# A fourth weight buffer, late list puts three a step, and the first batch's pooled remainder in the prologue of an attention and two-MoE kernel

## The chip, the cores and the metric

The kernel runs on 1 core of one Trainium2 chip. The metric is the device time of one execution in microseconds; lower is better. Before the change it is 747.93 us, the median of 3 runs.

## What is computed

An attention block is followed by two mixture-of-experts (MoE) layers. Cut to what matters:

```python
# q, k, v: (4, 8, 576, 64); factor = 4
q_d, k_d, v_d = (mean of each 4 neighbouring positions of q, k, v)
out_up = repeat(softmax(q_d k_d^T / 8) v_d, 4)           # pooled attention
out_local = softmax(q k^T / 8 where |i - j| < 4) v       # banded attention
x = out_up + out_local                                   # as 2304 rows of 512
x = moe(x, w_gate, w_output_gate, w1, w2)                # 8 experts, one per row
out = moe2(x, w_gate, w1, w2)

def moe(x, ...):
    e = argmax(x @ w_gate);  g = softmax(x @ w_gate)[e]
    y = relu(x @ w1[e]) @ w2[e]                          # 512 -> 1024 -> 512
    return g * sigmoid(x @ w_output_gate)[e] * y         # moe2 has no sigmoid
```

## The kernel before

**Attention** goes through 4 batches of 5 tiles, 20 tiles in all, in a loop over steps s (L818). In step s tile s gets its banded scores, tile s - 1 its probabilities transposed, its products with v and its 512 values a token (`xevac`, L681, which also stores the rows to `x0` in DRAM on SP's queue, two stores of at most 58 rows a tile), and tile s - 2 its gate logits (`xflip`, `lmm`, `lsel`). The pooled part of a batch is five `Pooled` objects: c = 0 to 3 take the first 128 pooled queries of a pair of heads, c = 4 the remainder, the last 16 to 32 of all pairs, in four column groups of TensorE. Each goes through `scores` (L502, the remainder's at L517 to L528) and `smax`, `exps`, `flip` and `evac`, `pvs` and `norm`. For later batches they are spread over the steps by `pooled_at` (L722). For batch 0, c = 0 to 3 are in the prologue, whose order is written out in `PRO` (s, m and f with a number stand for scores to exponential, transposes, and products with the norm); its remainder is in step `REM0` = 0 and the step after. GpSimd (POOL) makes the sums over four positions. The pooled v of a batch (`vpd`, L488) is needed by `pvs`.

**Routing.** When a group of tiles (`GROUPS`) has its logits, `route` (L256) finds each token's expert and place, and `spread` and `put` add the tokens to a list in PSUM: per tile `spread` makes `am`, `oc` and `bm` (L349 to L355; `bm` has two buffers, and `PB` says how many of its three parts are ACT operations at L353), and `put` is one matmul (L362). `ready1` and `puts1` (L836, L841) do one put and one spread a step, and `PUTN` = 2 of each from step 16 on. At the end of step 18 (`SNAP`) the tokens of the first 14 tiles are in the list, and `early` starts the first expert's work on 256 of them: `snap` picks the expert, `fetch` gathers the rows (`gather`, L1154) into `xr`, of which there are five buffers, and `prime` starts the weight loads. The tokens of the last six tiles come into the list after that; `rank` then orders the experts and a second `fetch` gathers 256 more rows for the second job, with the same weights.

**Experts.** `jobs` go through the experts of both layers. A job transposes its gathered rows (`xpose`, L1197: TensorE at L1206, ACT's upper half `xh` at L1216, VectorE's lower half `xl` at L1219), computes 8 hidden blocks (`hide`, three matmuls a product at L1294 to L1296; relu at L1420 and L1421), then the second layer. Each weight of 128 x 1024 is loaded on SP (`load_w`, L1085) into `raw`, of which there are `NRAW` = 3, split by `split_next` into `wh` (ACT cast, L1127) and `wl` (VectorE subtraction, L1135), and so gives its buffer free. `load_next` (L1095) issues a load when fewer than `NRAW` are loaded and not split. The weights of one expert are c = 0 to 7 in the stream, the first four for the first layer.

**Order.** The program order gives priorities, and a scheduler fixes each engine's instruction order before the run; each engine then works in order. Two ties are written by hand in `split_next`: the cast of c = 0 goes behind the last token's copy (`front`), the cast of c = `PINX` behind the first job's `xh` (`after`), and the subtraction of c = `PINX` behind the last tokens' places (`placed`, L326). The transposes of the first job go behind the last tokens' logits (`last`).

The engines are TensorE (PE), VectorE (DVE), ScalarE (ACT), GpSimd (POOL) and SyncE (SP, which issues the direct DMAs here). The functions that the diff touches:

Of the kernel before, what the change touches and what calls it, by code (L numbers as in the profile page):

```python
# [9 lines left out]
F32 = mybir.dt.float32  # L10
# [11 lines left out]
NP = H // 2  # L22
SD = S // 4
# [5 lines left out]
DM = 512  # L29
# [5 lines left out]
MAGIC = 12582912.0  # L35
NOV = 32
NWB = 9
NRAW = 3

CAPS = (  # L40
    (512, 384, 352, 320, 304, 288, 272, 256),
# [6 lines left out]
NWE = 3  # L48
POOLSPLIT = 0
POOLHI = 0  # L50
REM0 = 0
PUTN = 2
PB = (3, 2, 3, 2, 1)
PUTS = 15
PRI = 100
# [8 lines left out]
XA = 99  # L64
STEPF = {}
RLATE = 0
PINX = 4
QPE = 2
KPOOL = 0
Q1POOL = 0  # L70
S1 = "pppp"
PRO = "F0 s0 V0 s1 F2 s2 s3 zq m1 Ls m0 m2 f0 f1 lqk lvr f2 m3 V1 A0 lcs rep A2 f3 Le lvw zp lw1"
ORDER = "R As Ae q0f Cf Xt Cp p0s Xl Xs An p0e q1f p1s q0p Cx D p1e K q1p S"

C_ID = 0
# [105 lines left out]
def moe_pair_kernel(  # L181
# [212 lines left out]
    def attention(actx, early, early_x, front):  # L394
# [100 lines left out]
        class Pooled:  # L495
# [6 lines left out]
            def scores(self):  # L502
                b, c = self.b, self.c
                ps = psx.tile([128, 512], F32, tag="m", name="s")
                sv = ps[:, 0:2 * SD].rearrange("p (s k) -> p s k", s=2)
                if c < NP:
                    if b == 0 and c < QPE:
                        src = qt[b % 3][:, c, 0:512].rearrange("p (t r) -> p t r", r=4)
                        for r in range(4):
                            nc.tensor.matmul(  # L510
                                sv, lhsT=src[:, :, r], rhs=kpd[b % 2][:, :, c, :],
                                start=(r == 0), stop=(r == 3),
                            )
                    else:
                        nc.tensor.matmul(sv, lhsT=qd[b][:, c, 0:128], rhs=kpd[b % 2][:, :, c, :])
                else:
                    for a in range(NP):  # L517
                        if b == 0 and a < QPE:
                            src = qt[b % 3][:, a, S - 128:S].rearrange("p (t r) -> p t r", r=4)
                            ls = [src[:, :, r] for r in range(4)]  # L520
                        else:
                            ls = [qd[b][:, a, SD - 32:SD]]
                        for i, l in enumerate(ls):
                            nc.tensor.matmul(
                                sv[32 * a:32 * a + 32], lhsT=l,
                                rhs=kpd[b % 2][:, :, a, :], tile_position=(0, 32 * a),
                                start=(i == 0), stop=(i == len(ls) - 1), skip_group_check=True,
                            )  # L528
                self.sv = sv

            def smax(self):
# [190 lines left out]
        for b in range(B):  # L722
            s0 = NTP * (b - 1) + 2
            for c in range(NP + 1):
                if b or c == NP:
                    pooled_at.setdefault(s0 + c // 2 if b else REM0, []).append(Pooled(b, c))
        groups = GROUPS
        lgs_of = {}
        for g0, gn in groups:
# [29 lines left out]
        for i in range(3):  # L759
            t = sb3.tile([128, 3, 128], F32, tag="p", name="p")  # L760
            nc.sync.dma_start(t, crep[:, 3 * i:3 * i + 3])
            stg.append(t)
        c0 = [Pooled(0, c) for c in range(NP)]

        def start(c):
            c0[c].scores()
# [41 lines left out]
            "A0": lambda: sums1(0),  # L808
            "A2": lambda: sums1(2),
        }  # L810
        for c in range(NP):
            pro.update({
                f"s{c}": lambda c=c: start(c), f"m{c}": lambda c=c: middle(c), f"f{c}": lambda c=c: finish(c),
            })
# [155 lines left out]
    def experts():  # L970
# [7 lines left out]

        def pools_early():
            pool("raw", NRAW)  # L980
            pool("xr", 5)
            pool("x0")
            pool("w0", NWE)
            pool("h0")
# [181 lines left out]
        def fetch(job, fresh=None):  # L1166
# [10 lines left out]
            seen = tiles // NTP * S + tiles % NTP * 2 * GQ  # L1177
            x = []
            for k, mm in job.slots:
                xr = pl["xr"].tile([128, DM], F32, tag="xr", name="xr", bufs=5)  # L1180
                gather(M, xr, ri, k, mm, seen if job is M0.jobs[0] else NT)
                x.append(xr)
            job.x = x
# [121 lines left out]
        def overflow_slot(M, m, nov, i):  # L1305
# [39 lines left out]
            nc.vector.scalar_tensor_tensor(  # L1345
                ri[:, 0, 1:2], rf[:, 0, 0:1], -1.0, bg, op0=ALU.add, op1=ALU.add
            )
            xr = pl["xr"].tile([128, DM], F32, tag="xr", name="xr", bufs=5)
            gather(M, xr, ri, 0, 128)
            pt = psx.tile([128, 4, 128], F32, tag="m", name="t")  # L1350
            for d in range(4):
# [282 lines left out]
```

## Time and profile before

| | us |
|---|---|
| median of 3 runs | 747.93 |
| lowest, highest | 747.17, 748.26 |
| the profiled execution's own time | 742.5 |
| its span, first to last instruction | 740.7 |
| PE busy | 697.6 |
| DVE busy | 446.3 |
| ACT busy | 343.5 |
| POOL busy | 184.6 |

All times in the rows are microseconds from the start of the span, in the one profiled execution. A row of a timeline tells start, duration, engine, line, operation, what it writes and reads, shape and count; brackets at its end tell how long the engine stood idle just before and what ended that. PE's busy time contains waiting inside its pipeline.

### The profile page before, as it was taken

To read this page: it belongs to the slowest core of one execution; us is meant where nothing else is said; L and a number is where in the kernel's file an instruction comes from. 1 tells how busy PE (TensorE), PEld (TensorE's weight loads), DVE (VectorE), ACT (ScalarE), POOL (GpSimd) and SP (SyncE) were. 2 spreads that over 40 slices of the span, in tenths; PEclk is the share of its full clock that TensorE was granted. 3 is DMA by queue.
4 is the path that set the end of the run, shared out by engine and by line. 5 is a ranking of instruction groups with operands and counts; after the bars stand their busy time and mean duration, and the time that the engine had idled before them with its cause. 6 is when DMAs were issued, how large, how long until landed. Compare 5 with 4: busy or idle time off the path is not lost. (4 is left out here: it accounts for less than half of the span.)

```text
span 740.7 us, 15853 instructions
## 1 busy us (share of the span) xinstructions
PE 697.6 (94%) x6048; PEld 637.4 (86%) x6048; DVE 446.3 (60%) x1160; ACT 343.5 (46%) x634; POOL 184.6 (25%) x227
## 2 busy tenths in 40 slices
PE   8799899976989999999999999989999999999993
PEld 5468677765989999999999999878999999999992
DVE  7486979785667656575766776645444444555520
ACT  4055657584255353545454554155335354554620
POOL 5994720010131203121130130142013030321211
PEclk9699999996999999999999999999999999999998
DMA  9945553143176435445555461366435354565500
GB/s 354 420 140 210 184 196 132 55 156 131 58 247 207 160 121 183 140 161 179 173 176 168 141 221 59 110 213 217 128 111 182 126 186 141 176 193 178 163 21 16
DMA packets 52990, 120.99 MB, mean 163 GB/s; under 512 B 4800, under 2 KB 26176, under 8 KB 51884
## 3 DMA queue, kind: packets, MB, share of 16 engines
q1 hardware_dynamic: 45772, 99.19, 39.9%
q0 software_dynamic: 7136, 20.72, 8.2%
q8 instruction: 50, 0.82, 0.5%
q14 instruction: 32, 0.26, 0.1%
HBM read 101.01 MB, written 20.71 MB: 164 GB/s over the span
## 5 line engine op out<-in xcount | busy, mean ns | idle before, releaser
L1135 DVE TENSOR_TENSOR wl<-raw,wh 128x1024 fp32r<-128x1024 f32 x128 | 156.2, 1224 | 115.7 <-ACT wh L1127 115.4
L1127 ACT CAST wh<-raw 128x1024 fp32r<-128x1024 f32 x128 | 133.2, 1048 | 197.7 <-PE py L1295 113.3
L1294 PE MATMUL ph<-xh,wh 128*128 128x256 f32 (+8 forms) x576 | 172.3, 307 | 6.6 <-ACT xh L1216 6.6
L1295 PE MATMUL ph<-xl,wh 128*128 128x256 f32 (+8 forms) x576 | 175.6, 307 | 0.0
L1296 PE MATMUL ph<-xh,wl 128*128 128x256 f32 (+8 forms) x576 | 174.8, 305 | 0.0
L1294 PE MATMUL py<-h,wh 128*128 128x256 f32 (+8 forms) x448 | 138.4, 316 | 0.0
L1295 PE MATMUL py<-h,wh 128*128 128x256 f32 (+8 forms) x448 | 137.8, 311 | 0.0
L1296 PE MATMUL py<-h,wl 128*128 128x256 f32 (+8 forms) x448 | 137.4, 310 | 0.0
L1294 PEld LDWEIGHTS ph<-xh,wh 128*128 128x128 f32 x576 | 108.1, 190 | 8.4 <-ACT xh L1216 7.2
L1296 PEld LDWEIGHTS ph<-xh,wl 128*128 128x128 f32 x576 | 109.2, 190 | 0.6
L1295 PEld LDWEIGHTS ph<-xl,wh 128*128 128x128 f32 x576 | 109.1, 189 | 0.7
L1421 DVE SCALAR_TENSOR_TENSOR h<-ph,h 128x256 fp32r<-128x256 f32 (+8 forms) x144 | 66.2, 471 | 39.2 <-ACT h L1420 38.7
L1420 ACT ACTIVATE h<-ph 128x256 fp32r<-128x256 f32 (+8 forms) x144 | 60.7, 423 | 56.2 <-PE ph L1296 55.0
L1295 PEld LDWEIGHTS py<-h,wh 128*128 128x128 f32 x448 | 84.1, 188 | 0.6
L1296 PEld LDWEIGHTS py<-h,wl 128*128 128x128 f32 x448 | 84.1, 188 | 0.6
L1294 PEld LDWEIGHTS py<-h,wh 128*128 128x128 f32 x448 | 83.4, 188 | 0.9
L1156 POOL DMA_INDIRECT xr<-x,ri x49 | 50.3, 1026 | 97.1 <-PE t L1206 76.8
L1222 POOL DMA_INDIRECT out<-yr,ri x25 | 25.8, 1032 | 128.6 <-ACT yr L1240 84.2
L1222 POOL DMA_INDIRECT x<-yr,ri x24 | 25.1, 1044 | 126.3 <-ACT yr L1240 118.2
L1216 ACT CAST xh<-t 128x512 fp32r<-128x512 f32 (+5 forms) x49 | 26.1, 533 | 25.6 <-PE t L1206 25.5
L1494 DVE COPY yT<-py 128x256 f32<-128x256 f32 (+8 forms) x28 | 13.7, 490 | 39.9 <-PE py L1296 39.9
L1219 DVE TENSOR_TENSOR xl<-t,xh 128x512 fp32r<-128x512 f32 (+5 forms) x49 | 30.1, 620 | 10.5 <-ACT xh L1216 10.3
(194 smaller groups left out, 1041.8 us busy)
## 6 DMA issues: line engine op xcount, KB each, us to landing
raw<-w_a SPq DMA_DIRECT2D x64, 512.0 KB
raw<-w_b SPq DMA_DIRECT2D x64, 512.0 KB
vraw<-vr SPq DMA_DIRECT2D x4, 1560.0 KB
vd<-vw SPq DMA_DIRECT2D x4, 1280.0 KB
kd<-kT SPq DMA_DIRECT2D x8, 586.0 KB
qt<-qT SPq DMA_DIRECT2D x8, 586.0 KB
x<-zx SPq DMA_DIRECT2D x6, 768.0 KB
x<-x SPq DMA_DIRECT2D x36, 116.0 KB
```

The costliest lines, as they stand in the source:

```text
L1127: i = nc.scalar.copy(hi, raw)
L1135: i = nc.vector.tensor_tensor(lo, raw, hi.bitcast(F32), op=ALU.subtract)
L1156: g = nc.gpsimd.indirect_dma_start(xr[0:mm], None, src, bass.IndirectOffsetOnAxis(ap=ri[0:mm, k, 0:1], axis=0))
L1216: i = nc.scalar.copy(xh[:, :, o], pt[:, :, 0:mm])
L1219: nc.vector.tensor_tensor(xl[:, :, o], pt[:, :, 0:mm], xh[:, :, o].bitcast(F32), op=ALU.subtract)
L1222: i = nc.gpsimd.indirect_dma_start(M.dst[:, :], bass.IndirectOffsetOnAxis(ap=ri[0:mm, k, 1:2], axis=0), yr[0:mm], None, bounds_check=NT - ...
L1294: nc.tensor.matmul(ps, lhsT=ah, rhs=bh, start=first, stop=False)
L1295: nc.tensor.matmul(ps, lhsT=ah, rhs=bl, start=False, stop=False)
L1296: nc.tensor.matmul(ps, lhsT=al, rhs=bh, start=False, stop=last)
L1420: nc.scalar.activation(a[:, 0:n], ph[:, 0:n], func=AF.Relu)
L1421: nc.vector.scalar_tensor_tensor(b_[:, 0:n], ph[:, 0:n], 0.0, a[:, 0:n].bitcast(F32), op0=ALU.max, op1=ALU.subtract)
L1494: nc.vector.tensor_copy(yT[:, dc, 0:n], py[:, 0:n])
```

## The change

- `NRAW` goes from 3 to 4: four weight buffers. `xr` goes from five buffers to four.
- `PINX` goes from 4 to 3: the cast of the fourth weight (c = 3) goes behind the first job's `xh`, and its subtraction behind `placed`. The weight c = 4 loses these two ties.
- `PUTN` goes from 2 to 3: from step 16 on, up to three puts and three spreads a step.
- The remainder of batch 0 leaves steps 0 and 1 (`REM0` is removed) and enters the prologue as s4, m4, f4: its scores after the transposes of c = 2, its transposes after those of c = 3, its products behind the products of c = 3.
- The matmuls of the remainder's scores are issued in turns over the four column groups, instead of one group after the other. For batches after the first this leaves the order as it was.

```diff
-NRAW = 3
+NRAW = 4
...
-REM0 = 0
-PUTN = 2
+PUTN = 3
...
-PINX = 4
+PINX = 3
...
-PRO = "F0 s0 V0 s1 F2 s2 s3 zq m1 Ls m0 m2 f0 f1 lqk lvr f2 m3 V1 A0 lcs rep A2 f3 Le lvw zp lw1"
+PRO = "F0 s0 V0 s1 F2 s2 s3 zq m1 Ls m0 m2 s4 f0 f1 lqk lvr f2 m3 m4 V1 A0 lcs rep A2 f3 f4 Le lvw zp lw1"
...
+                    ls = []
                     for a in range(NP):
                         if b == 0 and a < QPE:
                             src = qt[b % 3][:, a, S - 128:S].rearrange("p (t r) -> p t r", r=4)
-                            ls = [src[:, :, r] for r in range(4)]
+                            ls.append([src[:, :, r] for r in range(4)])
                         else:
-                            ls = [qd[b][:, a, SD - 32:SD]]
-                        for i, l in enumerate(ls):
-                            nc.tensor.matmul(
...
+                            ls.append([qd[b][:, a, SD - 32:SD]])
+                    for i in range(4):
+                        for a in range(NP):
+                            if i < len(ls[a]):
+                                nc.tensor.matmul(
+                                    sv[32 * a:32 * a + 32], lhsT=ls[a][i],
...
-                if b or c == NP:
-                    pooled_at.setdefault(s0 + c // 2 if b else REM0, []).append(Pooled(b, c))
+                if b:
+                    pooled_at.setdefault(s0 + c // 2, []).append(Pooled(b, c))
...
-        c0 = [Pooled(0, c) for c in range(NP)]
+        c0 = [Pooled(0, c) for c in range(NP + 1)]
...
-            pool("xr", 5)
+            pool("xr", 4)
...
-                xr = pl["xr"].tile([128, DM], F32, tag="xr", name="xr", bufs=5)
+                xr = pl["xr"].tile([128, DM], F32, tag="xr", name="xr", bufs=4)
```

## Rows read from the trace of the kernel before

**Rows 1.** Stretch; us busy of PE, PEld, DVE, ACT, POOL; granted clock, DMA share, GB/s.

```profile
20.00:30.00 10.00, 5.86 (x22) 4.89 (x23) 4.50 (x10) 0.89 (x2) 9.48 (x12) 0.50 1.02 415
...
160.00:170.00 10.00, 5.42 (x73) 3.83 (x72) 8.67 (x40) 5.82 (x11) 2.66 (x5) 0.67 0.59 178
170.00:180.00 10.00, 3.70 (x15) 2.96 (x14) 4.95 (x22) 5.40 (x12) 0.00 (x0) 0.50 0.43 155
...
500.00:700.00 200.00, 200.00 (x1266) 191.58 (x1265) 98.67 (x131) 93.28 (x146) 39.62 (x45) 1.00 0.53 167
```

**Rows 2.** Timeline of PE at the border of attention and experts.

```profile
169.15 1.11 PE L1206 MATMUL t<-ident,xr 128*128 128x128 f32 x4 [0.37 <-DMA xr<-x,ri]
176.19 1.44 PE L1294 MATMUL ph<-xh,wh 128*128 128x256 f32 x5 [5.92 <-ACT xh L1216]
```

**Rows 3.** Timeline of ACT in the same stretch.

```profile
174.60 1.04 ACT L1127 CAST wh<-raw 128x1024 fp32r<-128x1024 f32 x1 [5.20 <-DMA raw<-w_a]
175.56 0.58 ACT L1216 CAST xh<-t 128x512 fp32r<-128x512 f32 x1
...
178.32 1.03 ACT L1127 CAST wh<-raw 128x1024 fp32r<-128x1024 f32 x1
...
181.43 0.20 ACT L309 ACTIVATE ez<-zs 128x2 f32<-128x2 f32 x1
```

**Rows 4.** Timeline of DVE from there on.

```profile
175.68 1.23 DVE L1135 TENSOR_TENSOR wl<-raw,wh 128x1024 fp32r<-128x1024 f32 x1 [4.98 <-ACT wh L1127]
...
185.47 0.16 DVE L326 TENSOR_TENSOR key<-key,cs 128x2 f32<-128x2 f32 x1
...
185.74 3.49 DVE L1135 TENSOR_TENSOR wl<-raw,wh 128x1024 fp32r<-128x1024 f32 x3
```

**Rows 5.** Timeline of SP's issues: the first weight loads and the last row stores.

```profile
153.25 1.55 SPq L1088 DMA_DIRECT2D raw<-w_a  x3
159.17 3.89 SPq L690 DMA_DIRECT2D x<-x  x4
165.61 21.82 SPq L1088 DMA_DIRECT2D raw<-w_a  x5
```

**Rows 6.** The same for single microseconds: stores alone, weights moving, before the late cast.

```profile
152.00:153.00 1.00, 0.93 (x12) 0.73 (x13) 0.97 (x4) 1.00 (x4) 0.00 (x0) 1.00 0.13 49
...
156.00:157.00 1.00, 1.00 (x24) 0.96 (x24) 0.76 (x2) 1.00 (x4) 0.00 (x0) 1.00 1.02 391
...
174.00:175.00 1.00, 0.00 (x0) 0.00 (x0) 0.00 (x0) 0.40 (x1) 0.00 (x0) 0.50 0.13 53
```

**Rows 7.** DMA issues: what, from where, count, size of one.

```profile
raw<-w_a SPq DMA_DIRECT2D x64, 512.0 KB
...
x<-x SPq DMA_DIRECT2D x36, 116.0 KB
```

**Rows 8.** Timeline of PE at the border of the two expert layers.

```profile
484.29 0.66 PE L1206 MATMUL t<-ident,xr 128*128 128x128 f32 x4 [1.81 <-DMA xr<-x,ri]
```

**Rows 9.** The second job's two gathers: the second issue, the landing times, PE's use.

```profile
198.66 0.94 POOL L1156 DMA_INDIRECT xr<-x,ri  x1 [0.31 <-issue]
...
DMA to landing us min/median/max: 3.4/3.8/4.1
...
202.90 0.60 PE L1206 MATMUL t<-ident,xr 128*128 128x128 f32 x4
```

**Rows 10.** Timelines of PE and POOL: batch 0's remainder, batch 1's pooled v and remainder.

```profile
30.38 3.99 PE L524 MATMUL s<-kpd,qt 128*32 128x288 f32 x13
...
35.03 0.39 PE L659 MATMUL v<-odh,rep 128*128 128x256 f32 x1
...
49.61 5.20 POOL L488 TENSOR_TENSOR vpd<-vraw 64x260 f32<-64x260 f32 x6
...
55.72 1.06 PE L564 MATMUL v<-vpd,pts 128*128 128x130 f32 x8
...
60.00 0.69 PE L524 MATMUL s<-kpd,qd 128*32 128x288 f32 x8
```

More of the change, by code (lines that the diff above doesn't have):

```diff
@@ L519, in scores @@
                             src = qt[b % 3][:, a, S - 128:S].rearrange("p (t r) -> p t r", r=4)
-                            ls = [src[:, :, r] for r in range(4)]
+                            ls.append([src[:, :, r] for r in range(4)])
                         else:
-                            ls = [qd[b][:, a, SD - 32:SD]]
-                        for i, l in enumerate(ls):
-                            nc.tensor.matmul(
[L525 to L528, printed above, removed]
+                            ls.append([qd[b][:, a, SD - 32:SD]])
[4 more added lines that the diff above has]
+                                    sv[32 * a:32 * a + 32], lhsT=ls[a][i],
+                                    rhs=kpd[b % 2][:, :, a, :], tile_position=(0, 32 * a),
+                                    start=(i == 0), stop=(i == len(ls[a]) - 1), skip_group_check=True,
+                                )
                 self.sv = sv
@@ L810, in attention @@
         }
-        for c in range(NP):
+        for c in range(NP + 1):
             pro.update({
@@ L1347, in overflow_slot @@
             )
-            xr = pl["xr"].tile([128, DM], F32, tag="xr", name="xr", bufs=5)
+            xr = pl["xr"].tile([128, DM], F32, tag="xr", name="xr", bufs=4)
             gather(M, xr, ri, 0, 128)
```

## The prediction

> **What bounds the kernel now.** I began with the table of busy time by stretch. TensorE (PE) is nearly always busy; the hole worth having is the border between attention and the first expert layer: in 160 to 180 us PE works 5.42 + 3.70 = 9.1 of 20 us, and the granted clock falls to 0.50, the lower of its two levels [rows 1]. The timeline of PE says where: the second transpose of the first job's rows runs at 169.15 us, and the first expert product (`hide`) starts at 176.19, after 5.92 us of idleness ended by ACT's `xh` (L1216) [rows 2].
>
> Next ACT's own timeline. The `xh` that PE waits for ran at 175.56, right behind a weight cast (L1127) that had stood 5.20 us for its load [rows 3]. ACT works in order: the fourth weight (c = 3) stood ahead of rows ready since about 170.3 (169.15 + 1.11). VectorE (DVE) stood too: its subtraction for the same weight waited 4.98 us, and the placing of the last tokens is queued behind it [rows 4].
>
> Why was that load late? SP issued three loads from 153.25, and the next only at 165.61, when the first buffer came free; between them lie the last row stores of attention (L690) [rows 5]. Ahead of the first load, while stores alone run, DMA is 0.13 busy at 49 GB/s: 0.13 of 16 is two engines; with weights moving it is 1.02 and 391 GB/s; at 174 to 175 us, with the fourth load still not landed, it is 0.13 and 53 GB/s again [rows 6]. So I read that this load ended on the two engines that the stores of 116 KB had held. A weight of 512 KB puts 32 KB on each of 16 engines, 64 KB on those two: 64 / 53 = 1.2 us each [rows 7]. Later PE has hardly a gap (500 to 700 us: 200.0 of 200, [rows 1]), but for the border between the two expert layers (1.81 us for the gathered rows, [rows 8]).
>
> **The change part by part.** All sums are against the profiled execution: 742.5 us, of which 740.7 are the span. The median of the runs is 747.93, 5.4 above it; I carry the difference over to it unchanged.
>
> *Fourth buffer and `PINX` = 3.* The fourth load is issued right behind the first three, some 11 us earlier, ahead of the last stores: at 391 GB/s 1.3 us more of transfer, then 1.2 us on the two engines. It is there before 169. Its cast is tied behind both `xh`, its subtraction behind the last tokens' places (`placed`). The later weights have no tie of their own, but in this trace they kept their order: the cast of c = 5 was over at 179.35 (178.32 + 1.03), yet no subtraction ran until that of c = 4, tied to `placed` (key at 185.47), opened the row of three at 185.74 [rows 3, 4]. So I expect c = 4 and later behind c = 3. Then `xh` runs at about 170.3, and PE starts at 170.3 + 0.6 = 170.9: 5.3 us earlier than 176.19. That is the upper end of this part.
>
> *What is late next.* The load that waited for the first free buffer still does; it is now that of c = 4. It is issued at 165.6 as before, behind the same stores, and one more weight lies on the two engines: it lands at 174.6 + 1.2 = 175.8. Its cast takes the place of the second cast after `xh` (178.32 in the trace); from there to the last tokens' second exponential (L309 at 181.43) are 3.11 us of ACT work [rows 3]. So that exponential comes at 175.8 + 3.1 = 178.9, only 2.5 us earlier. Queued behind this cast on ACT are the list's `bm`, that exponential and the first relu; DVE waits for the exponential before it places the last tokens, the list waits for them, and the second job's rows wait for the list. Those rows have no slack: the second gather is issued at 198.66, lands 4.1 us later at 202.8, and PE transposes it at 202.90 [rows 9]. With the list 2.5 us earlier they land at 200.3; PE, 5.3 us ahead, would be there at 197.6 and waits 2.7. The tied subtraction of c = 3 is needed for the seventh of eight `hide` steps; with `placed` at 183.0 (185.47 - 2.5) plus 1.2 it is ready at 184.2, about when PE comes to it, and what it costs lies inside the same 2.7. Between 2.5 and 5.3 I take the end that the two rows with the least slack give, -2.5.
>
> *Late puts, three a step.* Same spreads and puts, so no work is added; list buffers stay two, so the third spread starts when the first put is done. It can bring the first list, and gathers, up to about 1 us earlier (one spread is three ACT operations). PE cannot use it fully: rows go behind the last tokens' logits, and the hold on job 2 above is later anyway. I take 0, bounds -1 and +0.5 (a spread in front of a last tile's copy on ACT).
>
> *Remainder of batch 0 in the prologue.* Before, its scores (L524) run on PE from 30.38 to 35.03, 4.65 us, at the lower clock for the most part, with tile 0's first product (L659) queued behind [rows 10]. In 20 to 30 us PE is busy for 5.86 of 10 us and waits for POOL's pooled v [rows 1], so earlier scores are covered; were there no cover they would cost the same 4.65. Interleaving lets the four column groups work side by side, as batch 1's 8 do in 0.69 us [rows 10]; it shortens only what is hidden. The remainder's transposes and products still have to go before tile 0, some 1.5 us, and tile 0 needs the fourth pair's result at about 32. So 2.5 us at most are gained at 35 us. They meet POOL: the pooled v of batch 1 is finished at 49.61 + 5.20 = 54.81, and PE takes its last part at 55.72 [rows 10], a slack of 0.9. POOL's work is unchanged. Bounds 0 and -2.5 (PE can do other tiles meanwhile); I take -0.9, what the nearest row allows. DVE and ACT gain nothing in sum: the same operations, earlier.
>
> *Four row buffers (`xr`) instead of five.* A gather waits a transpose longer, with a whole job to spare; 0. *More loads ahead in the expert stages:* PE runs without gaps there, 0; at the second border one more load may stand ahead of the gathered rows, 0 to +1.3 (one load at 391 GB/s).
>
> [...]
>
> **Sum.** -2.5 - 0.9 = -3.4: 739.1 us profiled, 747.9 - 3.4 = **744.5 us** median. Its own range is 742.8 to 746.4.
>
> **The rivals.**
> A. *Nothing holds job 2.* If the fifth cast is queued behind the last exponential, or lands sooner, the whole 5.3 stands. For it: DVE's subtractions from c = 3 on are out of the way of the last tokens. Against it: casts stood between the list's work in the trace [rows 3]. 5.3 + 0.9 = 6.2 gives 741.7; with the prologue's 2.5, 740.1.
> B. *The wait is not removed.* If the fifth cast, which no tie holds, is queued between the two `xh`, as the fourth was, PE starts when it did. It speaks for this that its load is released at the same moment as the fourth's was; against it, that the later casts kept their order. With the prologue's 0.9 and nothing else: 747.0; up to 748 without.
> C. *Slower: one more weight stands ahead of what is waited for.* Same place as B, but the load lands 1.2 us later than before (175.8 against 174.6), and the second border's rows stand behind one more load, +1.3: 742.5 + 2.5 = 745.0, median 750.4; with the prologue's 0.9 749.5. It decides as soon as the fifth cast goes ahead of the second `xh` and the rows of the second border land later than for PE's 484.29 [rows 8].
>
> **How the numbers follow.** Forecast 0.50, A 0.22, B 0.17, C 0.11. A measurement of this kernel can tell about 0.2%, 1.5 us, from no change: under 746.4 is faster, over 749.4 slower. Faster: nearly all of the first two and a little of B, 0.73. Same: 0.16. Slower: 0.11. The range runs from the best of A (740.0) to 749.2, between B and C.
>
> **What would show it.** Right: a fourth load issued beside the three near 155 us; both `xh` together before 172, `hide` starting at about 171, ACT standing for a load until about 176 behind them, job 2's second transpose with a wait of some 2 us near 200, and L524 of batch 0 before 30 us. If that last wait is missing, it is A; if `xh` still stands until 175, B or C. What would make me wrong altogether: an order of DVE or ACT that puts a tied subtraction ahead of the last tokens, or a PE hole at 40 to 60 us where POOL is waited for longer than before.

## The result and the profile after

The changed kernel takes 751.15 us (median; 749.42 to 754.11), the kernel before beside it 746.43 us (745.51 to 748.26): a ratio of 1.0066, 95% interval 1.0049 to 1.0084. Forecast were 744.5 us, at most 749.2, and slower by over 0.2% had a chance of 0.11. The kernel became slower by some 4.7 us.

| | before | after |
|---|---|---|
| median | 746.43 us | 751.15 us |
| span of the profiled execution | 740.7 us | 748.6 us |
| time of the profiled execution | 742.5 us | 750.43 us |
| mean granted clock of TensorE | 0.972 | 0.966 |

The profiled executions differ by 7.9 us, more than the medians: that of the kernel before lies 3.9 us under its median, that of the kernel after 0.7. A part of the difference is stretches at a lower clock that a kernel of the old time shows too (0.83 as the mean of 10 us; below, at the run of the puts alone).

The table of stretches of the kernel after, to hold against [rows 1] (columns as there: stretch, length, busy time of PE, PEld, DVE, ACT, POOL with counts, granted clock, DMA share, GB/s), and under it three stretches of the kernel before that [rows 1] does not have:

```profile
50.00:60.00 10.00, 8.63 (x41) 7.98 (x41) 4.74 (x13) 1.89 (x4) 7.50 (x9) 0.66 0.45 160
170.00:180.00 10.00, 8.40 (x37) 7.46 (x37) 4.40 (x21) 3.75 (x7) 0.00 (x0) 0.55 0.50 181
200.00:215.00 15.00, 11.09 (x75) 9.60 (x74) 3.36 (x12) 3.82 (x7) 5.62 (x10) 0.77 0.47 150
485.00:500.00 15.00, 10.60 (x62) 9.31 (x61) 3.36 (x8) 4.59 (x8) 8.36 (x14) 0.77 0.62 205
```

```profile
50.00:60.00 10.00, 9.03 (x123) 7.50 (x121) 8.60 (x22) 4.55 (x10) 7.22 (x8) 1.00 0.98 363
200.00:215.00 15.00, 13.03 (x116) 12.42 (x115) 5.54 (x16) 5.96 (x12) 4.46 (x6) 1.00 0.59 192
485.00:500.00 15.00, 14.14 (x108) 13.51 (x109) 8.31 (x14) 8.02 (x14) 5.87 (x8) 1.00 0.66 196
```

What the change was for did happen: in 170 to 180 us PE is busy for 8.40 us instead of 3.70. But at 50 to 60, 200 to 215 and 485 to 500 us the granted clock is 0.66, 0.77 and 0.77 where before it was 1.00 (means over the stretch; taken in slices of 1 us it is 0.50 or 1.00 in all but 7 of 740 slices before and all but 12 of 740 after), and PE issues 41 matmuls instead of 123, 75 instead of 116, 62 instead of 108.

**A ledger of the 7.9 us**, made of the same five events in both traces. (1) The second transpose of the first job's rows, the end of attention: 171.54 against 169.15, +2.4. (2) The transpose of job 2's second rows: 205.09 against 202.90, so −0.2 in the border itself. (3) The first transpose at the second border: 488.71 against 484.29, +2.2 more. (4) The first expert product behind it: 493.03 against 486.52, +2.1 more. (5) The end of the span: 748.6 against 740.7, +1.4 more. The forecast had −0.9, −2.5, 0, 0 to +1.3, and 0.

**First border.** PE, ACT, DVE and POOL of the kernel after, to hold against [rows 2, 3, 4, 9]. A row is start, length, engine, line, operation, tiles, and in brackets the idle time before it and what ended it.

```profile
171.54 1.12 PE L1208 MATMUL t<-ident,xr 128*128 128x128 f32 x4 [0.35 <-DMA xr<-x,ri]
173.33 1.43 PE L1296 MATMUL ph<-xh,wh 128*128 128x256 f32 x5 [0.68 <-ACT xh L1218]
...
205.09 0.66 PE L1208 MATMUL t<-ident,xr 128*128 128x128 f32 x4 [1.37 <-DMA xr<-x,ri]
```

```profile
173.18 1.05 ACT L1129 CAST wh<-raw 128x1024 fp32r<-128x1024 f32 x1
178.37 1.05 ACT L1129 CAST wh<-raw 128x1024 fp32r<-128x1024 f32 x1 [4.14 <-DMA raw<-w_a]
179.32 0.72 ACT L352 ACTIVATE bm<-oc,v 128x144 fp32r<-128x144 f32 x2
179.94 1.03 ACT L1129 CAST wh<-raw 128x1024 fp32r<-128x1024 f32 x1
...
181.61 1.03 ACT L1129 CAST wh<-raw 128x1024 fp32r<-128x1024 f32 x1
182.54 0.20 ACT L308 ACTIVATE ez<-zs 128x2 f32<-128x2 f32 x1
```

```profile
186.22 0.15 DVE L325 TENSOR_TENSOR key<-key,cs 128x2 f32<-128x2 f32 x1
186.29 1.22 DVE L1137 TENSOR_TENSOR wl<-raw,wh 128x1024 fp32r<-128x1024 f32 x1
...
188.17 3.49 DVE L1137 TENSOR_TENSOR wl<-raw,wh 128x1024 fp32r<-128x1024 f32 x3
```

```profile
200.94 0.95 POOL L1158 DMA_INDIRECT xr<-x,ri  x1 [0.31 <-issue]
```

The fourth weight's cast (173.18) no longer stands ahead of `xh`, and the first product follows the transpose at once. The fifth weight's load, as forecast, is late in its stead: its cast waits 4.14 us with `bm` and the last exponential behind it. New is what DVE does after `key`: four subtractions (c = 3 and, behind one short operation of the ranks, three more) before the ranks go on, where [rows 4] had three.

**Prologue.** PE of the kernel after at 41 to 62 us and at 89 us, and POOL, to hold against [rows 10]; then three rows of the kernel before.

```profile
41.69 0.39 PE L611 MATMUL s<-cb 128*128 128x256 bf16 x2 [0.97 <-DVE p L632]
50.13 0.75 PE L514 MATMUL s<-kpd,qd 128*128 128x288 f32 x2 [0.88 <-DVE pd L538]
52.12 0.36 PE L661 MATMUL v<-odh,rep 128*128 128x256 f32 x1 [1.24 <-DVE p L632]
53.28 0.61 PE L669 MATMUL v<-od2h,rep 128*128 128x64 f32 x2
61.62 0.69 PE L526 MATMUL s<-kpd,qd 128*32 128x288 f32 x8
...
89.38 0.73 PE L361 MATMUL list<-bm,am 128*128 128x432 f32 x1 [4.16 <-ACT bm L352]
```

```profile
50.44 5.09 POOL L487 TENSOR_TENSOR vpd<-vraw 64x260 f32<-64x260 f32 x6
```

```profile
56.53 0.37 PE L659 MATMUL v<-odh,rep 128*128 128x256 f32 x1
57.45 0.39 PE L667 MATMUL v<-od2h,rep 128*128 128x64 f32 x2
...
87.02 0.47 PE L362 MATMUL list<-bm,am 128*128 128x432 f32 x1 [3.15 <-ACT bm L353]
```

After, tile 4's product at 52.12 comes 4.4 us ahead of its place before (56.53): the head start was there. But TensorE had run dry on the way (0.97, 0.88 and 1.24 us, waiting for DVE's softmax), POOL's pooled v is no earlier than before (50.44 + 5.09 = 55.53), and behind the third gap the clock is 0.50 (in each slice of 1 us from 53 to 59 us): a pair of L669 (L667 before) takes 0.61 instead of 0.39 us. At 61.62 the head start has become a lag of 1.6 us against the 60.00 of [rows 10]. A second wait makes it 2.4, the lag at the end of attention: at 89.38 the first list's put stands 4.16 us for ACT's `bm`, before 3.15 at 87.02.

**Second border.** PE and SP of the kernel after, to hold against [rows 8]:

```profile
488.71 0.66 PE L1208 MATMUL t<-ident,xr 128*128 128x128 f32 x4 [1.85 <-DMA xr<-x,ri]
491.24 1.12 PE L1208 MATMUL t<-ident,xr 128*128 128x128 f32 x4 [1.88 <-DMA xr<-x,ri]
...
484.74 18.76 SPq L1095 DMA_DIRECT2D raw<-w_b  x3
```

The second gather is 1.88 us late instead of 0.24. With four buffers a fifth load of the second layer (c = 76; in the one us from 488 us SP's queue moves 0.29 MB in 571 packets, some 512 bytes each) goes out at 484.74, between the issues of the two gathers (484.04 and 485.89); before, no such load was issued ahead of 492.38.

### The profile page after: what moved, and what is told of

It reads as the page before. It is cut to its first block, busy times and chain, and to the rows that moved or that the text cites. A ratio compares the mean times of both kernels' runs of the same rounds, so it can differ in the third digit from the quotient of the medians.

```text
span 748.6 us, 15846 instructions
## 1 busy us (share of the span) xinstructions
PE 702.6 (94%) x6048; PEld 644.3 (86%) x6048; DVE 446.6 (60%) x1160; ACT 342.9 (46%) x634; POOL 183.2 (24%) x227
## 5 line engine op out<-in xcount | busy, mean ns | idle before, releaser
L1297 PE MATMUL ph<-xl,wh 128*128 128x256 f32 (+8 forms) x576 | 177.4, 310 | 0.0
L1296 PE MATMUL ph<-xh,wh 128*128 128x256 f32 (+8 forms) x576 | 174.4, 311 | 1.4 <-ACT xh L1218 0.7
L1296 PEld LDWEIGHTS ph<-xh,wh 128*128 128x128 f32 x576 | 110.2, 194 | 3.8 <-issue 1.9
L1297 PEld LDWEIGHTS ph<-xl,wh 128*128 128x128 f32 x576 | 111.1, 193 | 0.6
L1298 PEld LDWEIGHTS ph<-xh,wl 128*128 128x128 f32 x576 | 111.0, 193 | 0.6
L1158 POOL DMA_INDIRECT xr<-x,ri x49 | 52.1, 1064 | 136.8 <-PE t L1208 108.4
```

The lines of the kernel that those rows point to most:

```text
L1158: g = nc.gpsimd.indirect_dma_start(xr[0:mm], None, src, bass.IndirectOffsetOnAxis(ap=ri[0:mm, k, 0:1], axis=0))
L1296: nc.tensor.matmul(ps, lhsT=ah, rhs=bh, start=first, stop=False)
L1297: nc.tensor.matmul(ps, lhsT=ah, rhs=bl, start=False, stop=False)
L1298: nc.tensor.matmul(ps, lhsT=al, rhs=bh, start=False, stop=last)
```

## The experiments

Ratios are to the kernel before on the same chip, with 95% intervals.

**Each part alone.** The prologue's lines alone; the buffers alone (`NRAW`, `PINX`, `xr`); the puts alone; the last two together.

```diff
 e1:  NRAW = 3, PINX = 4, xr bufs=5, PUTN = 2;  PRO and scores as after
 e2: -NRAW = 3      +NRAW = 4
     -PINX = 4      +PINX = 3
     -xr bufs=5     +xr bufs=4
 e3: -PUTN = 2      +PUTN = 3
 e4:  e2 and e3
```

> Of the change, the prologue part alone: the remainder of batch 0 as s4, m4, f4 in the prologue, its scores issued in turns over the column groups; three weight buffers, PINX 4, two puts a step as before. Theory now: TensorE gets ahead by some 2 to 3 us, runs out of work in front of batch 1's pooled v, which GpSimd finishes at about 55 us whatever happens, and the granted clock falls to 0.50 for some 7 us there; so slower by 1.0 to 2.5 us (ratio 1.001 to 1.003), with idle gaps near 50 us, clock 0.50 between 50 and 60 us and the rest of the trace shifted by that. Rival (the prediction's step): faster by 0.9 us (0.999). Rival 2: the prologue does nothing and all of the loss is in the weight buffers (1.000).

> Of the change, the buffers alone: four weight buffers, four row buffers, the fourth weight tied by PINX 3; prologue and puts as before. Theory now: hide starts 5 us earlier at the first border and all of it is lost again before the second job, whose rows come no earlier; there the idle time of TensorE brings a stretch at clock 0.50 (+1.7 us), and at the second border the fifth load's small packets stand between the two gathers (+2 us, and +1.4 for the clock): slower by 2 to 5 us (1.003 to 1.007). Rival (the prediction's step): faster by 2.5 us (0.9967). Rival 2: all of the loss is in the prologue, so 0.996 to 1.000.

> Of the change, three late puts a step alone. Theory: the same spreads and puts with the same two list buffers, 1.000 (within 0.7 us either way). Rival: the third spread stands in front of the last tiles' copies on ScalarE, slower by 0.5 to 1 us, with the last tokens' logits later by as much.

> The change without its prologue part: four weight buffers, four row buffers, PINX 3, three puts a step. Theory: as the buffers alone, slower by 2 to 5 us (1.003 to 1.007), less than the whole change by what the prologue alone costs (1 to 2.5 us). Rival: 0.996 to 1.000 if the prologue is the whole loss.

Measured: the prologue 1.0031 (1.0017 to 1.0045), the buffers 1.0027 (1.0016 to 1.0039), the puts 1.0007 (0.9992 to 1.0022), buffers and puts 1.0028 (1.0016 to 1.0039). The loss has two halves that add up to the change's 1.0066 within the intervals: 2.3 us for the prologue, 2.0 for the buffers, nothing that can be told for the puts.

The run of the puts alone, no slower than the kernel before, was profiled in an execution with a span of 743.4 us. Its stretches at the two places of the ledger's third and fifth terms, and the same of the kernel before:

```profile
205.00:215.00 10.00, 8.77 (x65) 8.36 (x66) 3.22 (x13) 3.95 (x8) 4.19 (x6) 0.83 0.78 253
485.00:495.00 10.00, 8.26 (x55) 7.79 (x56) 3.12 (x6) 3.27 (x6) 6.80 (x8) 0.83 0.57 181
```

```profile
205.00:215.00 10.00, 8.94 (x80) 8.53 (x81) 3.73 (x13) 4.41 (x9) 4.46 (x6) 1.00 0.77 257
485.00:495.00 10.00, 9.14 (x74) 8.84 (x75) 5.08 (x9) 4.98 (x9) 5.87 (x8) 1.00 0.56 168
```

So a lower clock at 205 and at 485 us is had by a kernel of the old time too, in some executions. The terms +2.2 and +1.4 of the ledger belong to the change only in part, which is how 7.9 us between two executions go with 4.7 between the medians.

**The first border: which hold keeps job 2's rows?** Two suspects: the fifth cast on ACT, and the one more subtraction on DVE. Three runs on top of the buffers alone: the fifth cast tied behind the last exponential (f1), the subtraction of c = 3 set free (f5), both (f4).

```diff
 f1, f4:
+    if c == 4:            # the cast of c = 4
+        for p in expl:    # behind the last tokens' second exponential
+            tc.add_manual_dep(i.ins, p.ins.name, NoSync)
 f4, f5:                   # tie of the subtraction to `placed`
-    if c == PINX:
+    if c == 4:
```

> Before plus the fourth buffer (as in the run of the buffers alone), with one more tie: the cast of c = 4 is queued behind the last tokens' second exponential. Theory (ACT's order gives the border back: the cast that waits for the fifth load holds the list's bm and the exponential): the 4 us wait of ACT is behind the exponential, which comes 4 to 5 us earlier than in the run of the buffers alone (near 176 instead of 181), the row of subtractions still stands ahead of the ranks, the second job's rows come 2 to 4 us earlier, ratio to before 0.998 to 1.001. Rival (the subtraction tied behind the last tokens' places decides, not ACT): the exponential earlier, the rows not, ratio 1.002 to 1.004.

> The fourth buffer with the subtraction of c = 3 set free (tied is that of c = 4), the fifth cast not tied. If ACT's wait for the fifth load and the one more subtraction ahead of the ranks each cost a part: the exponential as late as in the run of the buffers alone (near 181), the ranks about 1.2 us earlier, ratio 1.000 to 1.002. If the two were the same hold seen twice (either alone gives all): 0.992 as with both. If the subtraction's tie alone costs nothing: 1.0026 as in the run of the buffers alone.

> As the run with the fifth cast tied, and the subtraction of c = 3 set free: the tie behind the last tokens' places goes to that of c = 4. Theory (both hold the list): the subtraction of c = 3 runs in DVE's idle time before 180, the ranks come one subtraction (1.2 us) earlier than with the fifth cast's tie alone, ratio 0.996 to 0.999. Rival (only ACT's order counts): the same as with the fifth cast's tie alone, within 0.1%. Second rival (the free subtraction goes ahead of the last tokens' exponential's users on DVE and delays them): slower than with that tie alone by 1 us or more.

Measured, with places in us counted from the second transpose of the first job's rows (169.15 before, 171.54 after):

| kernel | first product | last exponential | `key` | second gather of job 2 | ratio |
|---|---|---|---|---|---|
| before | 7.04 | 12.28 | 16.32 | 29.51 | 1 |
| after | 1.79 | 11.00 | 14.68 | 29.40 | 1.0066 |
| buffers alone (e2) | 1.79 | 11.21 | 14.98 | 29.55 | 1.0027 |
| f5, subtraction free | 1.79 | 10.96 | 15.31 | 28.18 | 1.0025 (1.0011 to 1.0039) |
| f1, cast tied | 1.79 | 4.65 | 12.65 | 27.65 | 1.0000 (0.9989 to 1.0010) |
| f4, both | 1.79 | 5.84 | 9.39 | 23.74 | 0.9919 (0.9907 to 0.9932) |

The buffers alone bring the first product 5.3 us forward and the second gather not at all. Either repair alone brings the gather 1.4 to 1.9 us forward; in time f1 is back at the kernel before and f5 gains nothing. Both give 5.8 us of the gather, and with them a kernel that is faster than the one before (740.69 us). The profiled execution of f4 is the slowest of its six (745.33 us), but counted in this way the five other kernels with both repairs (below) agree with it: their second gather goes out at 23.57 to 24.86. I had expected a sum of two small gains and nothing better than 0.996. Why the two need each other is in the rows. First ACT and DVE of f1, then ACT of f4:

```profile
175.04 1.05 ACT L1128 CAST wh<-raw 128x1024 fp32r<-128x1024 f32 x1 [2.07 <-DMA raw<-w_a]
...
178.54 0.38 ACT L1428 ACTIVATE h<-ph 128x256 fp32r<-128x256 f32 x1
...
178.94 0.43 DVE L1429 SCALAR_TENSOR_TENSOR h<-ph,h 128x256 fp32r<-128x256 f32 x1 [2.33 <-ACT h L1428]
```

```profile
178.01 0.39 ACT L1428 ACTIVATE h<-ph 128x256 fp32r<-128x256 f32 x1 [1.53 <-PE ph L1304]
178.29 0.20 ACT L310 ACTIVATE ez<-zs 128x2 f32<-128x2 f32 x1
179.10 1.05 ACT L1128 CAST wh<-raw 128x1024 fp32r<-128x1024 f32 x1 [0.61 <-DMA raw<-w_a]
```

In f1 the exponential is out of the way of the fifth load, but the first relu is not: it stands behind the three casts (175.04 to 178.54), DVE's half of it (L1429) waits 2.33 us for it, and the placing of the last tokens is queued behind that. The wait had moved from one ACT operation to the next. In f4 the relu comes ahead of the cast: the other tie changed the whole order of ACT, and neither the last exponential nor the first relu waits for the load. Nearly all of f4's gain over the buffers alone lies ahead of `key` (9.39 against 14.98); from `key` to the gather it still takes 14.35 us, with later `bm` behind casts and four subtractions behind `key`. That f5's rows come 1.4 us earlier than those of the buffers alone without a gain in time is not explained.

**The second border: is it the fifth load?** Three runs were meant to hold it back, f6 on the buffers alone, f7 and f8 on f4:

```diff
 f6, f7:
-    if c >= len(stream) or c - nxt[1] >= NRAW:
+    if c >= len(stream) or c - nxt[1] >= (NRAW if c < 64 else 3):
 f8: f7, and the loads of c = 67 to 69 wait for the cast of c - 3
```

> Before plus the fourth buffer, but only three loads in flight from the second expert layer's first weight on (c of 64 and over). Theory (the extra load of a second-layer weight in 512-byte packets runs between the two gathers of the second border and delays the second, after which TensorE is at the lower clock for some 7 us): the second gap at the second border falls from 1.7 us to under 0.4, the granted clock stays at full speed there, and 2.0 to 3.4 us come back against the run of the buffers alone: ratio 0.998 to 1.000. Rival (the delay is handed on from the first border, the extra load is innocent): both gaps as in the run of the buffers alone, ratio 1.002 to 1.004.

> Fourth buffer, the fifth cast tied behind the last exponential, the subtraction of c = 3 set free, and three loads in flight from the second layer on. If the two borders' causes are the ones named, their gains add up: ratio 0.993 to 0.997, faster than both kernels, with the first expert product near 171. Rival (time at the first border is set by something that none of the edits moves, as the ranks' own chain): 0.998 to 1.000.

> The run with the fifth cast tied and the subtraction of c = 3 free, and now a wait that truly keeps the second layer's fifth weight back: its load waits for the cast three weights before it, as in the kernel before (holding back the order of the program alone left the load where it was, near 482 us, in the run that tried it). Theory (that load, in 512-byte packets, runs among the gathered rows and delays the second gather): the 512-byte packets come after 490 us, the second gap of the second border is under 0.4 us, no half-clock stretch follows it, and 1.5 to 3 us come back against the run with tie and free subtraction (ratio to before 0.988 to 0.990). Rival (load innocent; the gap is the gather's own latency): the same 0.992.

Measured: f6 1.0026 (1.0015 to 1.0038), f7 0.9956 (0.9939 to 0.9973), f8 0.9951 (0.9934 to 0.9969). None of the three moved the load: it goes out at 482.39, 475.56 and 475.66, still between the gathers. f6 and f7 change only the load's place in the order of the program, and with four buffers nothing makes SP wait at that place. f8 has a true wait, but for c = 67 to 69, weights of the layer's first expert that are issued some 40 to 60 us before the border; the border's load is c = 76. So the three do not test the question. They show that holding the loads back from c = 64 on costs f4 some 0.3% (the intervals are apart); why is open. The right load, on top of f4:

```diff
 f10:
-    if c >= len(stream) or c - nxt[1] >= NRAW:
+    if c >= len(stream) or c - nxt[1] >= (3 if c == 76 else NRAW):
+    if c == 76:           # its load waits for the cast of c = 73
+        tc.add_manual_dep(load.ins, casts[c - 3].ins.name, Sync)
```

> The run with the fifth cast tied and the subtraction of c = 3 free, and the load of c = 76 (the second border's fifth in flight, in 512-byte packets) made to wait for the cast three weights before it, as in the kernel before. Theory (that load among the gathered rows delays the second gather, and the idleness brings a half-clock stretch): the load is issued after 485 us, the second gap of the border falls from 1.16 us to 0.3 us or less, the half-clock stretch behind it is gone or half as long, ratio 0.987 to 0.990 (against 0.992). Rival (the load is innocent): 0.992 with both gaps as they were.

Measured: 0.9901 (0.9878 to 0.9923), 737.63 us: faster than the kernels before and after, and the lowest median here, though its interval overlaps that of f4. PE at this border and the clock of it, first f4, then f10, and the clock of i2 (below), which has the same wait:

```profile
484.05 0.66 PE L1214 MATMUL t<-ident,xr 128*128 128x128 f32 x4 [2.16 <-DMA xr<-x,ri]
485.86 1.11 PE L1214 MATMUL t<-ident,xr 128*128 128x128 f32 x4 [1.16 <-DMA xr<-x,ri]
484.00:494.00 10.00, 8.12 (x46) 7.48 (x47) 1.92 (x5) 2.68 (x5) 5.29 (x7) 0.66 0.56 183
```

```profile
478.57 0.66 PE L1221 MATMUL t<-ident,xr 128*128 128x128 f32 x4 [1.16 <-DMA xr<-x,ri]
479.99 0.66 PE L1221 MATMUL t<-ident,xr 128*128 128x128 f32 x4 [0.77 <-DMA xr<-x,ri]
475.00:490.00 15.00, 12.40 (x90) 11.11 (x89) 5.02 (x13) 5.97 (x11) 8.90 (x14) 1.00 0.58 189
```

```profile
479.75:489.75 10.00, 8.65 (x46) 8.18 (x47) 2.28 (x5) 2.88 (x5) 5.61 (x8) 0.66 0.52 159
```

With the load behind the border (it is issued at 487.94) both gaps are smaller in f10, 1.16 and 0.77 against 2.16 and 1.16 us. The traces of all kernels here, the ones below among them, say how far this can be put down to the load. Gaps are PE's two waits for gathered rows at this border, in us; the clock is the mean of the 10 us from the first transpose:

| where the load of c = 76 is | kernels | second gap | both gaps together | clock |
|---|---|---|---|---|
| behind the border, three buffers | before, e1, e3, h1, h2, p1, p2, i1 | 0.24 or less | 1.9 to 2.4 | 1.00 in five, 0.66 to 0.83 in e1, e3, p2 |
| between the gathers, four buffers | after, e2, e4, f1, f4 to f8 | 1.09 to 1.88 | 3.2 to 3.7, f7 5.1 | 0.51 to 0.83 in all nine |
| made to wait, four buffers | f10, i2, q1 | 0.68 to 0.82 | 1.9 to 2.2 | 1.00 in f10, 0.66 in i2 and q1 |

So the load between the gathers costs some 1.4 us of waits at this border (both gaps 3.32 in f4, 1.93 in f10), and holding it back gives them back. The second gap isn't down to the 0.3 that I had expected; with four buffers the four loads before it go out within 2.06 us (6.16 before), and whether they hold the gather was not tried. The clock of 1.00 in f10 can't be put down to the load: i2 and q1, with the same wait, have 0.66 there, and three kernels without the load 0.66 to 0.83. Nor do the times of f4 and f10, whose intervals overlap, show a gain. The second gap is over 1 us in every trace with the load between the gathers, and 0.24 us or less in every one with three buffers; in what way the load holds the gathered rows back, no trace here shows.

**The prologue: what eats the head start?** The suspect named in the prediction was POOL's pooled v of batch 1. Its first additions left out, so that it sums two of four rows, with the prologue's change (h1) and without (h2); then the same order of POOL's work changed with nothing left out, the sums of batch 2 behind that pooled v, with (p1) and without (p2).

```diff
 h1, h2: in sums_v
+    if b != 1:
         eng.tensor_tensor(vraw[:, k, 0:2], vraw[:, k, 0:2], vraw[:, k, 2:4], op=ALU.add)
 p1, p2: in sums_k and sums_q, the additions of b == 2
+    tc.add_manual_dep(i.ins, vlast[0].ins.name, NoSync)   # last pooled v of batch 1
```

> The prologue's change alone, with POOL's first additions for the pooled v of the second batch left out (the three L484 of that batch, some 3.8 to 4.2 us of POOL; the pooled v then sums two of four rows). Theory (TensorE, ahead by 3 to 4 us, runs dry at 50 to 55 us because POOL's pooled v is no earlier, and then falls to the lower clock): the idleness at 50 to 53 us and the half-clock stretch behind it are gone, ratio 0.995 to 1.000. Rival (POOL isn't what is waited for; DVE and the score order are): the stretch stays, ratio 1.002 to 1.004.

> The kernel before with the same three additions left out, as the control. Theory (before, POOL's pooled v came 0.9 us ahead of its use, so nothing waits for it): 0.999 to 1.001. Rival (POOL's later work is late all through attention): under 0.998.

> The prologue's change alone, with no work left out, but POOL's order changed: the pooled sums of k and q of the third batch (b = 2) are tied behind the pooled v of the second, whose load has landed near 38.5 us while POOL begins on it at 43.8. Theory (TensorE runs dry because POOL's pooled v is queued behind work that nobody needs yet): the pooled v is done near 48 to 50 instead of 55, the half-clock stretch at 51 to 62 us is gone, ratio to before 0.994 to 0.998. Rival (less work on POOL was the gain of the cut, not its order): the third batch's sums are late in turn, 1.000 to 1.004.

> The control: the kernel before with only that order of POOL. If the prologue's change needs the earlier pooled v and gains by it, this run lies 1.5 to 2.5 us above the one with the change: ratio 0.997 to 1.000. If the order alone is the gain, the two are equal.

Measured: h1 0.9941 (0.9921 to 0.9960) against h2 0.9969 (0.9953 to 0.9985); p1 1.0018 (1.0002 to 1.0035) against p2 1.0017 (1.0002 to 1.0032). With POOL's work shorter the prologue's change gains by its medians what I had forecast as its best, 743.59 − 741.13 = 2.5 us (the two intervals overlap a little); the control, expected at 1, gained 0.3% by itself. The stretch 50 to 60 us of the prologue alone, then of h1, and the gap of p1:

```profile
50.00:60.00 10.00, 8.76 (x41) 8.33 (x39) 4.20 (x11) 1.44 (x3) 6.94 (x8) 0.57 0.50 184
```

```profile
50.00:60.00 10.00, 9.90 (x139) 8.45 (x139) 5.91 (x15) 4.59 (x10) 4.92 (x6) 1.00 0.58 214
```

```profile
43.82 0.39 PE L628 MATMUL s<-cb 128*128 128x256 bf16 x2 [1.93 <-DVE p L649]
40.00:50.00 10.00, 7.44 (x94) 5.92 (x90) 9.47 (x18) 4.17 (x8) 9.58 (x11) 0.74 0.51 182
```

In h1 TensorE stays busy (9.90 of 10 us) and the clock at 1.00, and the head start is kept. In p1 POOL's pooled v is done at 48.7 us instead of 55, yet TensorE idles 1.93 us at 43.8 for DVE's softmax, and the clock is lower there instead (0.74 at 40 to 50 us, 1.00 in the prologue alone). So the gate is not POOL alone, and my theory of the two p runs (0.994 to 0.998) was wrong: with the new order the moved remainder costs nothing that can be told (p1 against p2), but both are slower than the kernel before. The new order has a price of its own, which p2 shows: at 91.83 PE stands 5.23 us, for DVE's `pd` of the batch whose sums were put back.

```profile
91.83 2.94 PE L581 MATMUL v<-vpd,pts 128*128 128x130 f32 x12 [5.23 <-DVE pd L553]
```

One trace shows the same loss without any change of the prologue. In the profiled execution of f4, whose engines go through attention in the order of the kernel before, the clock rose sooner (1.00 at 30 to 35 us, 0.63 before), and TensorE began tile 0 at 32.42 instead of 35.03 [rows 10]:

```profile
32.42 0.38 PE L660 MATMUL v<-odh,rep 128*128 128x256 f32 x1
...
172.45 1.12 PE L1214 MATMUL t<-ident,xr 128*128 128x128 f32 x4 [0.60 <-DMA xr<-x,ri]
```

It then waits for POOL's pooled v (0.74 us at 54.66) and for DVE (0.98 at 70.94, 1.74 at 90.26), the clock is 0.50 at 90 to 95 us (0.83 before), and the second transpose runs at 172.45, 3.3 us later than in the kernel before [rows 2]. A head start of 2.6 us at tile 0 can so end in a loss wherever it comes from; it is one execution, and nobody set its clock.

**Interleaved or moved?** The interleaved order of the remainder's scores alone, in the place it had before:

```diff
 i1: scores() as after;  PRO, REM0 and c0 as before
```

> The kernel before with only the new order of the matmuls in the remainder's scores (four column groups in turn), the remainder where it was, in step 0. Theory (any head start of TensorE at 35 us ends in waits for VectorE's softmax at 43 to 52 us and a half-clock stretch behind them): the scores take 2 us instead of 4.65, tile 0 starts some 2 us earlier, a half-clock stretch of 3 to 10 us stands between 44 and 62 us, ratio 1.001 to 1.004. Rival (the moved transposes and products of the remainder are what costs): no such stretch, the 2 us are kept at least in part, ratio 0.997 to 1.000.

Measured: 0.9987 (0.9974 to 0.9999). My theory failed: the scores (L527) take 4.1 us from 30.15 to 34.2, not the expected 2, and the clock at 40 to 60 us is 1.00. The rival holds in its time; its reason is not shown. Of 0.9 us at tile 0 (34.14 against 35.03) 0.2 are left at tile 4 (56.3 against 56.5), and the gain comes at 86 us, where the first list's put waits 2.02 us for `bm` instead of 3.15. There POOL's order is another too, with a pair of its sums (`kpd`) ahead, at 60.6 us, so the run isn't the interleaving alone. Shown is that the loss in the prologue comes with the moving of the remainder ahead of tile 0 (e1 against i1, intervals apart).

**All repairs together.** The change with ties, wait and POOL's new order (q1, without the puts), and f10 with the interleaved scores in place of the moved remainder (i2).

```diff
 q1: after with PUTN = 2, and the edits of f4, f10 and p1
 i2: f10 and i1
```

> The change without its puts, with all repairs: fifth cast tied behind the last exponential, subtraction of c = 3 free, the second border's fifth load waiting, POOL's pooled v of the second batch ahead of the third's sums. If the causes are those named and add up: the sum of the run with the load's wait and of the prologue with the new order, ratio 0.982 to 0.987. If one of them only seemed to help: no better than the run with the load's wait alone, 0.987 to 0.992.

> Fourth buffer, fifth cast tied behind the last exponential, subtraction of c = 3 free, the second border's fifth load waiting, and the interleaved order of the remainder's scores in its old place. If the gains of the two runs add up: 0.9901 x 0.9987 = 0.989, range 0.987 to 0.991. If the interleaving costs here: 0.992 or more.

Measured: q1 0.9942 (0.9924 to 0.9959), i2 0.9910 (0.9877 to 0.9944). q1 is slower than f10 by 0.4%, as much as the moved remainder costs against the interleaving alone (1.0031 − 0.9987); moved remainder and POOL's new order together are a loss still. i2 can't be told from f10.

## Why the prediction was wrong, point by point

*"5.3 us earlier than 176.19".* Right to 0.1 us: from transpose to first product 1.79 instead of 7.04. The load of c = 4 was late as worked out (cast at 175.8 forecast; 178.37 less attention's 2.4 is 176.0). The puts at 0 were right, and rivals B and C failed as it expected: the fifth cast did not go ahead of the second `xh`. All signs that the prediction named for being right came (four loads from 155.83, both `xh` begun by 172.69, ACT standing until 178.37, the remainder's scores before 30 us, a wait of 1.37 for job 2's rows), and the time did not: these signs test the mechanism, not its price.

*"So that exponential comes ... only 2.5 us earlier."* Wrong size: 1.28. I let 3.11 us pass from the fifth cast to the exponential, the row of the cast that I took to be replaced; in the trace after, three casts stand between (178.37 to 182.54), 4.17 us.

*"... what it costs lies inside the same 2.7."* This is the step that failed at the border. The tied subtraction of c = 3 was weighed against its own user, the seventh `hide` step, and not against what is queued behind it on DVE: the rank chain that ends in the list. One more subtraction of 1.22 us there ate the rest: from `key` to the gather 14.72 instead of 13.19 us (with only that tie moved on to c = 4, f5 against e2, 12.87 instead of 14.57). So −2.5 became −0.1 to −0.2. From the first product to the second transpose of job 2 PE takes 31.76 us instead of 26.71, before and then after:

```profile
176.19:202.90 26.71, 26.33 (x202) 25.59 (x203) 18.96 (x78) 10.72 (x26) 2.42 (x5) 0.92 0.19 61
```

```profile
173.33:205.09 31.76, 28.61 (x208) 27.46 (x208) 19.79 (x79) 11.87 (x28) 2.41 (x5) 0.91 0.17 59
```

Of the 5.05 us more, 2.8 are idleness (1.37 of it for the rows) and 2.3 busy time, for 208 matmuls against 202 at a clock of 0.91 against 0.92; what that busy time is made of is open. The end was taken from the two rows with the least slack; both lay on one chain, and their costs add.

*"Bounds 0 and −2.5 (PE can do other tiles meanwhile); I take −0.9."* The second failed step: a loss was left out with no reason that excludes one. In its place e1 cost 2.3 us. The prediction did name a hole at 40 to 60 us, with a longer wait for POOL, as what would make it wrong altogether, but gave it no price; the hole came, its three waits ended by DVE. Its price, in rows at either clock (0.50 after, 1.00 before): seven pairs of L669 2.99 us instead of 1.56 before (52.85 to 55.84, 57.23 to 58.79), which makes 1.4; the same pairs take 0.39 us each in h1.

*"0 to +1.3 (one load at 391 GB/s)."* Right place, too small: 1.64 us by the second gap (1.88 against 0.24), and a stretch at a clock of 0.50 followed (each slice of 1 us from 491 to 496 us), in which the second rows' transposes take 1.12 instead of 0.66 us.

Common to the second, third and fourth: the sum priced waits by their length. Behind the wait of 1.24 us at 52.12 the clock was 0.50, and the seven pairs above took 1.4 us more, about as much again. That the idleness brings the lower clock is an inference, and the length of the waits alone does not tell when: at the second border 1.81 and 0.24 us leave the clock at 1.00 in the kernel before, 1.96 and 0.19 us are followed by 0.83 in e1; 1.16 and 0.77 us leave it at 1.00 in f10, 1.18 and 0.82 us are followed by 0.66 in q1. No run changed the clock by itself.

Of the rivals, none came as told. C had the right sign and, by its second half, the second border, one of the right places; its first half did not occur.

## What to carry to other kernels

When a buffer takes a late load out of one wait, the next load can inherit the lateness (here the fifth weight's cast stood 4.14 us in place of the fourth's 5.20): follow it through every operation behind it on the engine that waits, to the last user, and do it again after each repair; here the gain came only when neither the last exponential nor the first relu stood behind the load any more. A tie that orders one operation behind another has a price for all that is queued behind it, not only for its own user (here one subtraction of 1.22 us, and 14.72 instead of 13.19 us from `key` to the gather). The head start of one engine was worth nothing here, where its suppliers did not start earlier too (4.4 us ahead at tile 4, 1.6 us behind at 61.62); where one ends in idleness, look for the clock behind it, and price what runs at the lower one (here 0.61 instead of 0.39 us a pair).

## What was not expected of the hardware

Gaps of TensorE of 0.9 to 1.9 us, each far shorter than the 5.92 us at [rows 2], were followed by stretches at a lower clock (0.57 to 0.77 as the mean of 10 to 15 us), though not always, and kernels of the same time differ in which of these stretches their profiled executions have (the kernel before and the puts alone, at 205 and 485 us). Even with the same order of work in attention its end lies 3.8 us apart (second transpose at 168.62 in f8, 172.45 in f4). A sum over one profiled execution can so be off by 3 us (7.9 against 4.7 here) without any term of it being wrong.
